# One visit a tile for the local attention jobs on TensorE, and ScalarE's activation moved to the head of a step, in a fused attention and feed-forward kernel

## The chip, the cores and the metric

The kernel runs on one core of one Trainium2 chip. The metric is the device time of one execution in microseconds (us), lower is better. Everything is computed in float32 precision: the large matmuls take each float32 operand as the sum of two float32r parts, a high one and the rest.

## The reference

Eight heads of sparse attention over eight sequences of 576 tokens, then a feed-forward layer over all 4608 tokens. The first four heads are local (a token sees itself and the 31 before it), the last four are strided (a token sees the earlier ones with the same position modulo 32).

```python
rel = pos[:, None] - pos[None, :]
mask_local = (rel >= 0) & (rel < 32)
mask_strided = (rel >= 0) & (pos[None, :] % 32 == pos[:, None] % 32)
masks = np.stack([mask_local if h < H // 2 else mask_strided for h in range(H)], axis=0)
scores = np.where(masks[None], (q @ k.transpose(0, 1, 3, 2)) / np.sqrt(D), -1e9)
attn = np.exp(scores - scores.max(-1, keepdims=True))
attn = attn / (attn.sum(-1, keepdims=True) + 1e-9)
x = (attn @ v).transpose(0, 2, 1, 3).reshape(B * S, H * D)      # 4608 x 512
h = x @ w_in                                                    # 512 x 2048
out = (0.5 * h * (1.0 + erf(h / np.sqrt(2.0)))) @ w_out         # 2048 x 512
```

## The kernel before

The tokens are cut into 12 tiles of 384, the feed-forward width into 16 blocks of 128. A step n is one tile and one block (n = 16 * tile + block, 192 steps). In a step `ffn_h(n)` issues 12 matmuls of 384 columns (4 channel groups, three products of high and low parts each: L602 to L604) into a PSUM tile `H`, of which there are two. `ffn_g(n)` makes the gate: the Gelu on ScalarE (L611, "the activation" below), a rounded copy `gh` on ScalarE (L613), and the rest `gl = H - gh` on VectorE (L615). `ffn_o(n - 2)` issues 9 matmuls of 512 columns (L641 to L643) into three PSUM banks. So TensorE runs H(n), O(n-2), H(n+1), O(n-1), H(n+2), and H(n+2) needs the bank of H(n), which is free once `gl` of step n is made.

The input x of a tile (`x_tile`: a high and a low part, two buffers) is made by attention while the tile before it is in the feed-forward. Its strided half comes from VectorE, row by row, in units of up to four rows: products of q and k (L477), maximum and subtraction (L485, L486), the exponential on ScalarE (L487), sums and quotients (L503 to L507), weighted sums of v (L517, L519), a transpose `xs` (L527). The units stand in one long list, `strided`; `run_strided(upto)` issues from it up to a cost given by the step, with the costs that stand beside each operation, so that a tile's units are done about two steps before the tile starts. An exponential is put on a list `exps` and issued by `flush_exps`, in the loop either at the unit's sum (`zsum`) or in the part of a local job that has exponentials of its own. A finished unit leaves a "split" on the list `splits`: a copy of `xs` into x's high part on ScalarE (L230) and the rest on VectorE (L232), in `to_x`.

The local half comes from three jobs a tile (`band_job`, parts 0 to 6, run by `part`): 0 scores (32 matmuls a job in the trace, L290) into the banks S0 and S1; 1 mask and row minimum on VectorE (L304); 2 four exponentials on ScalarE (L308); 3 sum, reciprocal, quotient and transpose on VectorE (L311 to L314) and eight small transfers into a band matrix; 4 values (16 matmuls a job, L328) into the bank X (the third job: S0); 5 and 6 `to_x`. `visit(n)` at the head of a step runs parts 0 and 1 of the three jobs in block 2 of a tile, parts 2 and 3 in the steps after it (a job every other step), and parts 4 to 6 in block 12, all for the next tile.

The first 16 steps are woven by hand with the loading of the weights and the first tiles' attention (`START`); the loop from step 16 on calls `step(n)`. In the loop the order on ScalarE and TensorE is that of the program; on VectorE, GpSimd and the transfer queue of SP a planner orders by its own estimate of when each instruction is ready.

Of the kernel before, what the change touches and what calls it, by code (L numbers as in the profile page):

```python
# [10 lines left out]
F32 = mybir.dt.float32  # L11
# [12 lines left out]
P = 128  # L24
STRIDE = 32
TT = 384
LU = 64
# [55 lines left out]
def attn_ffn_kernel(ctx: ExitStack, tc: tile.TileContext, qk, vl, qka, va, qs, ks, vs, w, out):  # L83
    nc = tc.nc
    NJ = qk.shape[0]
    NR, D = qs.shape[2:]
    S = NR * STRIDE
    HL = P // STRIDE
    NT, DM = out.shape
    NF = w.shape[0]  # L90
    NC = DM // P
    NU = len(PLACE)
    NV = len(VISITS)
    NTILE = NT // TT
    NS = NTILE * NF
    JPT = NJ // NTILE
    SC = 1.0 / (D ** 0.5)
    DH = D // 32
    N2 = HL // 2
# [11 lines left out]
    ps_a = ctx.enter_context(tc.tile_pool(name="ps_a", bufs=1, space=bass.MemoryType.PSUM))  # L111
# [8 lines left out]
    def rows(j):  # L120
        return slice(j * D, (j + 1) * D)
# [4 lines left out]
    def slot(name, shape, dtype=F32):  # L126

        return wpool.tile(shape, dtype, name=name, tag="w")
# [41 lines left out]
    def x_tile(t):  # L170
        if t not in xt:
            xt[t] = [xpool.tile([P, NC, TT], F32R, name=f"x{i}_{t}", tag=f"x{i}{t % 2}") for i in "hl"]
        return xt[t]


    jq, jv = {}, {}
# [8 lines left out]
    def load_jv(x):  # L185
        if x < NJ and ("v", x) not in loaded:
            loaded.add(("v", x))
            jv[x] = lpool.tile([LK, 2, HL, D], F32, name=f"vl_{x}", tag="vl", bufs=4)
            nc.sync.dma_start(jv[x], vl[x])
# [8 lines left out]
    def small(name):  # L198
        return [lpool.tile([P, 4], F32, name=f"{k}_{name}", tag=k, bufs=4) for k in ("nm", "ss", "rs")]
# [29 lines left out]
    def to_x(dh_, dl_, src):  # L229
        nc.scalar.copy(dh_, src)  # L230
        yield
        nc.vector.tensor_tensor(dl_, src, dh_.bitcast(F32), ALU.subtract)  # L232

    def local_job(x, banks=None, dve=0, pn=-1):
# [35 lines left out]
        dst = [a[:, 0:N2, c0:c0 + P] for a in x_tile(t)]  # L270
        yield from to_x(*dst, xv)

    def band_job(x, bt, sx=None):

        QB = STRIDE
        i = x % JPT if sx is not None else 0
        sx = {} if sx is None else sx
        if i == 0:  # L280
            sx["s"] = [ps_a.tile([P, DM], F32, name=f"S{j}_L{x}", tag=f"S{j}") for j in range(2)]
        s = [t[:, i * P:(i + 1) * P] for t in sx["s"]]
        qv = jq[x][:, 0:2 * N2 * LU].rearrange("p (r a t) -> p r a t", r=N2, a=2)
        kv = jq.pop(x)[:, 2 * N2 * LU:].rearrange("p (r a t) -> p r a t", r=N2, a=2)
        head = [(h % 2, slice(h // 2 * 2 * QB, (h // 2 + 1) * 2 * QB)) for h in range(HL)]
        for h in range(0, HL, 2):
            for g in range(P // QB):
                a, b = divmod(g, 2)
                for j in range(2):
                    nc.tensor.matmul(s[j][g * QB:(g + 1) * QB, head[h][1]],  # L290
                                     qv[rows(j), h // 2, a, b * QB:(b + 1) * QB],
                                     kv[rows(j), h // 2, a, b * QB:(b + 2) * QB],
                                     start=True, stop=True, tile_position=(j * D, g * QB))
        yield
        p1 = lpool.tile([P, 4 * LK], F32, name=f"P_L{x}", tag="P", bufs=2)
        p2 = lpool.tile([P, DM], F32, name=f"PT_L{x}", tag="PT", bufs=2)
        pb, pt = p2[:, 0:DM // 2], p2[:, DM // 2:]
        pv = pb.rearrange("p (c h t) -> p c h t", c=2, h=HL)
        nm, ss, rs = small(f"L{x}")
        first_ = [a for a in range(2) if LPLACE[2 * x + a][1] == 0]  # L300
        msk = bmask[first_[0] if first_ else None]
        for h in range(HL):
            j, cs = head[h]
            nc.vector.tensor_tensor_reduce(p1[:, h * 2 * QB:(h + 1) * 2 * QB], s[j][:, cs], msk, -SC, 3.0e38,  # L304
                                           ALU.add, ALU.min, nm[:, h:h + 1])
        yield
        for h in range(HL):
            nc.scalar.activation(pv[:, :, h, :], p1[:, h * 2 * QB:(h + 1) * 2 * QB].rearrange(  # L308
                "p (c t) -> p c t", c=2), AF.Exp, bias=nm[:, h:h + 1], scale=-1.0, accum_out=ss[:, h:h + 1])
        yield  # L310
        nc.vector.tensor_scalar_add(ss, ss, 1e-9)  # L311
        nc.vector.reciprocal(rs, ss)
        nc.vector.tensor_tensor(pv, pv, rs.unsqueeze(1).unsqueeze(3).to_broadcast([P, 2, HL, QB]), ALU.mult)
        nc.vector.transpose(pt, pb)  # L314
        tv = pt.rearrange("p (c q) -> p c q", c=2)
        for g in range(P // QB):
            for c in range(2):
                kb = g % 2 + c
                nc.sync.dma_start(bt[kb * QB:(kb + 1) * QB, g, :], tv[g * QB:(g + 1) * QB, c, :])
        yield  # L320
        if i % 2 == 0:
            sx["x"] = ps_a.tile([P, DM], F32, name=f"X_L{x}", tag="X" if i == 0 else "S0")
        xv = sx["x"][:, i % 2 * N2 * P:(i % 2 + 1) * N2 * P].rearrange("p (r q) -> p r q", r=N2)
        bv = bt.rearrange("p (a b) (h q) -> p a b h q", a=2, h=HL)
        for r in range(N2):
            for a in range(2):
                for j in range(2):
                    nc.tensor.matmul(xv[rows(j), r, a * LU:(a + 1) * LU], jv[x][:, a, 2 * r + j, :],  # L328
                                     bv[:LK, a, :, 2 * r + j, :], start=True, stop=True)
        jv.pop(x)  # L330
        load_jv(x + 3)
        yield
        t, c0 = divmod(x * P, TT)
        dst = [d[:, 0:N2, c0:c0 + P] for d in x_tile(t)]
        yield from to_x(*dst, xv)


    ka = {}
# [90 lines left out]
    for vi in range(NA, NV):  # L429
        n = VISITS[vi][2]  # L430
# [26 lines left out]
    exps, splits = [], []  # L457

    def flush_exps(u):
        while exps and exps[0][0] <= u:  # L460
            exps.pop(0)[1]()
# [132 lines left out]
    ready = [t * NF for t in range(NTILE)]  # L594
    xfree = [0, 0] + ready[1:-1]
# [58 lines left out]
    N0 = 17  # L654
    U0 = sum(x[4] <= NA for x in PLACE)
    for u in range(U0, NU + 1):
        for v, what, names in ((u, strided_qk, "qk"), (u - 1, strided_av, "v")):
            if U0 <= v < NU:
                vi, _, r0, nr, t, _ = PLACE[v]
# [3 lines left out]
    cum, last = [], [0.0] * NTILE  # L663
    tot = 0.0
# [6 lines left out]
    def run_strided(upto):  # L671
        while pos[0] < len(strided) and cum[pos[0]] <= upto + 1e-9:
            if strided[pos[0]][1] == 0.6 and len(splits) >= 3:
                break
            strided[pos[0]][2]()
            pos[0] += 1

    pbig = []
    t = slot("pbig", [P, 4 * DM])
# [35 lines left out]
    for i in range(JPT):  # L715
        t = opool.tile([P, DM], F32, name=f"first_{i}", tag="ob", bufs=3)
# [34 lines left out]
    with tc.manual_schedule(engines={ET.DVE, ET.Activation, ET.PE, ET.SP}):  # L751
        for it in START:
            kind = it[0]
            if kind in "wqvSBEe":
                x = int(it[1:] or 0)
# [12 lines left out]

    SCORES, VALUES = 2, 12
    score_at = {ready[t - 1] + SCORES: t for t in range(2, NTILE)}
    value_at = {ready[t - 1] + VALUES: t for t in range(2, NTILE)}
    banks = {}
    local = {}
    band = slot("band", [P, 4 * DM])
# [4 lines left out]
    def part(x, *which):  # L781

        for p in which:
            if p == 0:
                local[x] = [band_job(x, bts[x % NBT], banks), 0]
            assert local[x][1] == p
            local[x][1] += 1
            if next(local[x][0], True) is not None:
                load_jq(x + 3)

    def visit(n):

        for i in range(JPT):
            for d, p in ((1, 2), (2, 3)):
                t = score_at.get(n - 2 * i - d)
                if t is not None:
                    if p == 2:
                        flush_exps(NU)
                    part(t * JPT + i, p)
        if n in score_at:  # L800
            for p in (0, 1):
                for i in range(JPT):
                    part(score_at[n] * JPT + i, p)
        if n in value_at:
            for ps in ((4,), (5, 6)):
                for i in range(JPT):
                    part(value_at[n] * JPT + i, *ps)

    def step(n):
        c = n // NF  # L810
        while splits and n >= xfree[splits[0][0]]:
            for _ in splits.pop(0)[1]():
                pass
        visit(n)
        if c + 1 < NTILE:
            a, e = ready[c] + (1 if c == 0 else 0), ready[c + 1]
            need = last[c] + (last[c + 1] - last[c]) * min(1.0, max(0.0, (n - a + 1) / (e - a - 2)))
            run_strided(max(need, tot * (n - N0) / (ready[-1] - 2 - N0)))
        if NB <= n < NS:
            ffn_h(n)  # L820
            for _ in ffn_g(n):
                pass
        if n == NS + 1:
            ffn_o(n - 3, n - 2)
        elif n >= NB + 2 and n < NS:
            ffn_o(n - 2)
        if n >= NB + 2 and (n - 2) % NF == NF - 1:
            store((n - 2) // NF)

    with tc.manual_schedule(engines={ET.Activation, ET.PE}):  # L830
        for n in range(NB, NS + 1):
            step(n)
# [67 lines left out]
```

## Time and profile before

| | before |
|---|---|
| median of three runs | 886.04 us (886.02 to 887.12) |
| the profiled execution | 886.71 us, of which the span from first to last instruction 884.8 |
| granted TensorE clock, mean | 0.999 |
| TensorE matmul busy | 861.5 us, 97% of the span |
| VectorE busy | 713.9 us, 81% |
| ScalarE busy | 457.5 us, 52% |
| mean of one: Gelu (L611), its copy (L613), `gl` (L615) | 475, 480 and 554 ns |
| mean of one: `to_x` of a local job on ScalarE (L230), on VectorE (L232) | 376 and 417 ns |
| median from issue to landing: q and k of a job, a band transfer | 4.6 and 1.8 us |

A row of the timeline gives the start of an instruction in us from the span's start, its duration, engine, line, operation, what it writes and reads, and in brackets how long its engine sat idle before it and what ended that. Consecutive instructions of one kind are merged (x48). Matmuls overlap in their pipeline, so the pace of TensorE is read from the starts, not from the durations.

### The profile page before, as it was taken

To read this page: it belongs to the slowest core of one execution; us is meant where nothing else is said; L and a number is where in the kernel's file an instruction comes from. 1 tells how busy PE (TensorE), PEld (TensorE's weight loads), DVE (VectorE), ACT (ScalarE), POOL (GpSimd) and SP (SyncE) were. 2 spreads that over 40 slices of the span, in tenths; PEclk is the share of its full clock that TensorE was granted. 3 is DMA by queue.
4 is the path that set the end of the run, shared out by engine and by line. 5 is a ranking of instruction groups with operands and counts; after the bars stand their busy time and mean duration, and the time that the engine had idled before them with its cause. 6 is when DMAs were issued, how large, how long until landed. Compare 5 with 4: busy or idle time off the path is not lost.

```text
span 884.8 us, 19306 instructions
## 1 busy us (share of the span) xinstructions
PE 861.5 (97%) x5984; PEld 771.1 (87%) x5984; DVE 713.9 (81%) x4897; ACT 457.5 (52%) x975; POOL 17.9 (2%) x89
## 2 busy tenths in 40 slices
PE   5699999999999999999999999999999999999998
PEld 4488898989989889889898988988888998999997
DVE  5999899599969999849989969969979988675111
ACT  5999574256546357247336436436534632733222
POOL 5000100000000000000000000000000000000000
PEclk9999999999999999999999999999999999999999
DMA  9981420221030122102012122012113011100001
GB/s 335 343 342 36 148 85 16 81 82 46 28 134 14 60 71 77 34 21 97 21 66 87 40 75 87 14 54 82 60 34 108 13 60 37 27 20 1 36 1 36
DMA packets 34551, 66.66 MB, mean 75 GB/s; under 512 B 6800, under 2 KB 16528, under 8 KB 32400
## 3 DMA queue, kind: packets, MB, share of 16 engines
q1 hardware_dynamic: 34448, 65.43, 22.3%
q8 instruction: 47, 0.77, 0.3%
q14 instruction: 56, 0.46, 0.2%
HBM read 51.64 MB, written 9.44 MB: 69 GB/s over the span
## 4 chain that ended last, share of the span: by engine, by line
PE 92%; DVE 5%; POOL 1%; issue 1%; ACT 0%; DMA 0%; SPq 0%; POOLq 0%; DVEq 0%
PE H L602 15%; PE H L604 15%; PE O L642 15%; PE O L643 15%; PE H L603 15%; PE O L641 14%; PE X_L L328 2%; PE S_L L290 1%; DVE acc L519 1%; DVE ws L153 1%; DVE junk L477 1%; DVE w L163 0%; DVE ws L155 0%; DVE P_L L304 0%; POOL bmask L697 0%
## 5 line engine op out<-in xcount | busy, mean ns | idle before, releaser
L611 ACT ACTIVATE H<-H 128x384 f32<-128x384 f32 x192 | 91.2, 475 | 355.8 <-PE H L604 303.2
L602 PE MATMUL H<-xh,w 128*128 128x384 f32 x768 | 262.7, 342 | 2.4 <-ACT xh L230 1.2
L604 PE MATMUL H<-xh,w 128*128 128x384 f32 x768 | 260.7, 339 | 1.7 <-DVE w L163 1.7
L603 PE MATMUL H<-xl,w 128*128 128x384 f32 x768 | 259.6, 338 | 0.7 <-DVE xl L232 0.7
L519 DVE SCALAR_TENSOR_TENSOR acc<-sv,sc,acc 128x64 f32<-128x64 f32 x1158 | 253.8, 282 | 0.6
L643 PE MATMUL O<-w,gl 128*128 128x512 f32 x576 | 228.2, 396 | 0.0
L642 PE MATMUL O<-w,gh 128*128 128x512 f32 x576 | 227.9, 396 | 0.0
L641 PE MATMUL O<-w,gh 128*128 128x512 f32 x576 | 224.7, 390 | 0.0
L477 DVE CUSTOM_DVE_ANT_0 junk<-sq,sk 128x64 f32<-128x64 f32 x1290 | 209.7, 219 | 7.3 <-DMA sk<-in_ks_dram 7.3
L615 DVE TENSOR_TENSOR gl<-H,gh 128x384 fp32r<-128x384 f32 x192 | 106.4, 554 | 110.0 <-ACT gh L613 109.0
L602 PEld LDWEIGHTS H<-xh,w 128*128 128x128 f32 x768 | 145.3, 189 | 12.8 <-ACT xh L230 1.4
L603 PEld LDWEIGHTS H<-xl,w 128*128 128x128 f32 x768 | 145.3, 189 | 8.4 <-DVE xl L232 1.1
L604 PEld LDWEIGHTS H<-xh,w 128*128 128x128 f32 x768 | 145.1, 189 | 2.3 <-DVE w L163 2.2
L643 PEld LDWEIGHTS O<-w,gl 128*128 128x128 f32 x576 | 108.3, 188 | 23.1
L642 PEld LDWEIGHTS O<-w,gh 128*128 128x128 f32 x576 | 108.3, 188 | 18.2
L641 PEld LDWEIGHTS O<-w,gh 128*128 128x128 f32 x576 | 108.5, 188 | 17.5
L477 DVE DVE_READ_ACCUMULATOR2_ANT sc<- 128x1 f32 x1290 | 107.0, 83 | 0.0
L613 ACT CAST gh<-H 128x384 fp32r<-128x384 f32 x192 | 92.2, 480 | 6.0
L611 ACT ACT_TABLE_LOAD x47 | 60.3, 1283 | 0.8
L487 ACT ACT_TABLE_LOAD x35 | 44.9, 1283 | 0.6
L308 ACT ACTIVATE PT_L<-P_L,nm_L 128x64 f32<-128x64 f32 x132 | 44.0, 335 | 0.1
L517 DVE TENSOR_SCALAR acc<-sv,sc 128x64 f32<-128x64 f32 x132 | 26.5, 264 | 1.5 <-DMA sv<-in_vs_dram 1.2
(106 smaller groups left out, 500.0 us busy)
## 6 DMA issues: line engine op xcount, KB each, us to landing
ws<-in_w_dram SPq DMA_DIRECT2D x16, 1024.0 KB, 11.2
qk<-in_qk_dram SPq DMA_DIRECT2D x36, 320.0 KB, 4.6
out_dram<-ob SPq DMA_DIRECT2D x34, 256.0 KB, 2.5
vl<-in_vl_dram SPq DMA_DIRECT2D x36, 192.0 KB, 3.2
sk<-in_ks_dram SPq DMA_DIRECT2D x8, 576.0 KB, 4.6
sv<-in_vs_dram SPq DMA_DIRECT2D x8, 576.0 KB, 3.9
band<-PT_L SPq DMA_DIRECT2D x240, 16.0 KB, 1.8
sq<-in_qs_dram SPq DMA_DIRECT2D x4, 576.0 KB, 4.2
```

The source lines that it names most:

```text
L477: nc.vector.tensor_tensor_reduce(junk, sq[vi, "q"][:, r0 + r, :], sq[vi, "k"][:, c, :], 1.0, 0.0, ALU.mult, ALU.add, ss[u][:, r, c:c + 1])
L487: exps.append((u, lambda: nc.scalar.activation(s, s, AF.Exp, scale=SC)))
L519: nc.vector.scalar_tensor_tensor(acc[:, r, :], sq[vi, "v"][:, c, :], wgt, acc[:, r, :], ALU.mult, ALU.add)
L602: nc.tensor.matmul(hp, w1[f][:, 0, c, :], xh[:, c, :], start=(c == 0), stop=False)
L603: nc.tensor.matmul(hp, w1[f][:, 0, c, :], xl[:, c, :], start=False, stop=False)
L604: nc.tensor.matmul(hp, w1[f][:, 1, c, :], xh[:, c, :], start=False, stop=(c == NC - 1))
L611: nc.scalar.activation(hp, hp, AF.Gelu)
L613: nc.scalar.copy(gh, hp)
L615: nc.vector.tensor_tensor(gl, hp, gh.bitcast(F32), ALU.subtract)
L641: nc.tensor.matmul(o, gh[:, sl], w2[f][:, 0, :], start=(f == 0), stop=False)
L642: nc.tensor.matmul(o, gh[:, sl], w2[f][:, 1, :], start=False, stop=False)
L643: nc.tensor.matmul(o, gl[:, sl], w2[f][:, 0, :], start=False, stop=(f == NF - 1))
```

## The change

`visit(n)` now runs, in block 13 of a tile, part 4 (values) of the next tile's three jobs and right behind them part 0 (scores) of the three jobs of the tile after that; only the first loop tile's scores have a visit of their own. The third job's values go into the last 128 columns of the two banks that the scores behind them are about to fill. Parts 1 to 3 are spread over 11 steps, a job every four steps (every two for the first tile), and parts 5 and 6 follow in the step of the visit; all of these come from a new `softmaxes(n)`. In `step(n)` the H matmuls and the gate now stand ahead of the splits, the local jobs' parts, a `flush_exps` of every exponential outstanding, and the strided list; the strided list's pace is set to end one step earlier. The next q and k of a job are loaded at part 0 and not after part 6.

```diff
+    def score_banks(t):
+        return [ps_a.tile([P, DM], F32, name=f"S{j}_{t}", tag=f"S{j}") for j in range(2)]
...
-        if i == 0:
-            sx["s"] = [ps_a.tile([P, DM], F32, name=f"S{j}_L{x}", tag=f"S{j}") for j in range(2)]
-        s = [t[:, i * P:(i + 1) * P] for t in sx["s"]]
+        sx = {x // JPT: score_banks(x // JPT)} if sx is None else sx
+        s = [t[:, i * P:(i + 1) * P] for t in sx[x // JPT]]
...
-        if i % 2 == 0:
-            sx["x"] = ps_a.tile([P, DM], F32, name=f"X_L{x}", tag="X" if i == 0 else "S0")
-        xv = sx["x"][:, i % 2 * N2 * P:(i % 2 + 1) * N2 * P].rearrange("p (r q) -> p r q", r=N2)
+        if i == 0:
+            sx["x"] = ps_a.tile([P, DM], F32, name=f"X_L{x}", tag="X")
+
+        xv = [sx["x"][:, (N2 * i + r) * P:(N2 * i + r + 1) * P] if i < 2 else sx[x // JPT + 1][r][:, JPT * P:]
+              for r in range(N2)]
...
-        yield from to_x(*dst, xv)
+        if i < 2:
+            both = [(sx["x"][:, i * N2 * P:(i + 1) * N2 * P].rearrange("p (r q) -> p r q", r=N2), slice(0, N2))]
+        else:
+            both = [(xv[r], r) for r in range(N2)]
+        parts = [to_x(*[w_[:, d, c0:c0 + P] for w_ in x_tile(t)], src) for src, d in both]
...
-    SCORES, VALUES = 2, 12
-    score_at = {ready[t - 1] + SCORES: t for t in range(2, NTILE)}
-    value_at = {ready[t - 1] + VALUES: t for t in range(2, NTILE)}
+    FIRST, VISIT = 2, 13
+    value_at = {ready[t - 1] + VISIT: t for t in range(2, NTILE)}
+    score_at = {ready[1] + FIRST: 2, **{n: t + 1 for n, t in value_at.items()}}
+    soft_at = {}
+    for n, t in score_at.items():
+        for i in range(JPT):
+            for p in (1, 2, 3):
+                soft_at.setdefault(n + p + i * (2 if t == 2 else 4), []).append((t * JPT + i, p))
...
-            if next(local[x][0], True) is not None:
+            next(local[x][0], None)
+            if p == 0:
                 load_jq(x + 3)
...
+        t = value_at.get(n, 0)
         if n in score_at:
-            for p in (0, 1):
-                for i in range(JPT):
-                    part(score_at[n] * JPT + i, p)
-        if n in value_at:
-            for ps in ((4,), (5, 6)):
-                for i in range(JPT):
-                    part(value_at[n] * JPT + i, *ps)
+            banks[score_at[n]] = score_banks(score_at[n])
+        for i in range(JPT if t else 0):
+            part(t * JPT + i, 4)
+        for i in range(JPT if score_at.get(n, NTILE) < NTILE else 0):
+            part(score_at[n] * JPT + i, 0)
+
+    def softmaxes(n):
+
+        t = value_at.get(n, 0)
+        for i in range(JPT if t else 0):
+            part(t * JPT + i, 5, 6)
+        for x, p in soft_at.get(n, ()):
+            if x < NJ:
+                if p == 2:
+                    flush_exps(NU)
+                part(x, p)
 
     def step(n):
         c = n // NF
-        while splits and n >= xfree[splits[0][0]]:
-            for _ in splits.pop(0)[1]():
-                pass
         visit(n)
-        if c + 1 < NTILE:
-            a, e = ready[c] + (1 if c == 0 else 0), ready[c + 1]
-            need = last[c] + (last[c + 1] - last[c]) * min(1.0, max(0.0, (n - a + 1) / (e - a - 2)))
-            run_strided(max(need, tot * (n - N0) / (ready[-1] - 2 - N0)))
         if NB <= n < NS:
             ffn_h(n)
             for _ in ffn_g(n):
                 pass
+        old = len(splits)
+        while old and n >= xfree[splits[0][0]]:
+            for _ in splits.pop(0)[1]():
+                pass
+            old -= 1
+        softmaxes(n)
+        flush_exps(NU)
+        if c + 1 < NTILE:
+            a, e = ready[c] + (1 if c == 0 else 0), ready[c + 1]
+            need = last[c] + (last[c + 1] - last[c]) * min(1.0, max(0.0, (n - a + 1) / (e - a - 3)))
+            run_strided(max(need, tot * (n - N0) / (ready[-1] - 3 - N0)))
```

## Rows read from the trace of the kernel before

**Rows 1.** Timeline of PE around one values visit, from step 43 on

```profile
225.34 0.33 PE L602 MATMUL H<-xh,w 128*128 128x384 f32 x1
...
229.62 1.62 PE L328 MATMUL X_L<-band,vl 96*64 96x64 f32 x48
231.17 0.44 PE L602 MATMUL H<-xh,w 128*128 128x384 f32 x1
...
235.46 0.33 PE L602 MATMUL H<-xh,w 128*128 128x384 f32 x1
...
239.65 0.33 PE L602 MATMUL H<-xh,w 128*128 128x384 f32 x1
```

**Rows 2.** Timeline of PE around one scores visit, step 34

```profile
182.16 0.33 PE L602 MATMUL H<-xh,w 128*128 128x384 f32 x1
...
186.45 1.17 PE L290 MATMUL S_L<-qk 64*32 64x64 f32 x96
187.55 0.45 PE L602 MATMUL H<-xh,w 128*128 128x384 f32 x1
...
191.84 0.33 PE L602 MATMUL H<-xh,w 128*128 128x384 f32 x1
```

**Rows 3.** Timeline of PE in the opening: values and scores side by side

```profile
54.45 0.69 PE L328 MATMUL X_L<-first,vl 96*64 96x64 f32 x16
55.07 0.45 PE L290 MATMUL S_L<-qk 64*32 64x64 f32 x32
55.45 0.44 PE L602 MATMUL H<-xh,w 128*128 128x384 f32 x1
```

**Rows 4.** Timeline of PE in the opening: a job's values alone

```profile
93.91 0.69 PE L328 MATMUL X_L<-first,vl 96*64 96x64 f32 x16
94.52 0.50 PE L641 MATMUL O<-w,gh 128*128 128x512 f32 x1
```

**Rows 5.** Waits of the whole run: who waited for whom, us, times, longest

```profile
ACT xh L230 <- DVE xs L527: 14.3, 5, 6.4
...
DVE z L503 <- ACT sc L487: 12.4, 15, 1.1
...
PE H L602 <- DVE gl L615: 0.9, 1, 0.9
```

**Rows 6.** Timeline of ACT before and in the slow step 134

```profile
619.65 1.28 ACT L308 ACT_TABLE_LOAD   x1
...
623.69 0.47 ACT L611 ACTIVATE H<-H 128x384 f32<-128x384 f32 x1
...
631.08 0.41 ACT L230 CAST xh<-xs 128x256 fp32r<-128x256 f32 x1 [6.40 <-DVE xs L527]
631.39 0.47 ACT L611 ACTIVATE H<-H 128x384 f32<-128x384 f32 x1
```

**Rows 7.** Timeline of PE at its one wait, before step 136

```profile
626.64 0.33 PE L604 MATMUL H<-xh,w 128*128 128x384 f32 x1
...
628.90 0.33 PE L602 MATMUL H<-xh,w 128*128 128x384 f32 x1
...
634.17 0.44 PE L602 MATMUL H<-xh,w 128*128 128x384 f32 x1 [0.92 <-DVE gl L615]
...
638.46 0.33 PE L602 MATMUL H<-xh,w 128*128 128x384 f32 x1
```

**Rows 8.** Groups by line on ACT from 117 us on: busy, mean, idle before

```profile
L611 ACT ACTIVATE H<-H 128x384 f32<-128x384 f32 x175 | 83.1, 475 | 343.0 <-PE H L604 294.3 <-DVE sc L477 24.6 <-DVE acc L519 12.8
...
L487 ACT ACT_TABLE_LOAD x34 | 43.6, 1283 | 0.6
...
L308 ACT ACT_TABLE_LOAD x10 | 12.8, 1283 | 0.2
...
L487 ACT ACTIVATE sc<-sc 128x32 f32<-128x32 f32 (+9 forms) x34 | 8.1, 239 | 0.4
```

**Rows 9.** Busy time in one stretch of 70 us: PE, PEld, DVE, ACT, POOL

```profile
186.00:256.00 70.00, 70.00 (x482) 63.00 (x481) 66.74 (x551) 36.68 (x81) 0.66 (x5) 1.00 0.21 66
```

More of the change, by code (lines that the diff above doesn't have):

```diff
@@ L278, in band_job @@
         i = x % JPT if sx is not None else 0
-        sx = {} if sx is None else sx
-        if i == 0:
-            sx["s"] = [ps_a.tile([P, DM], F32, name=f"S{j}_L{x}", tag=f"S{j}") for j in range(2)]
-        s = [t[:, i * P:(i + 1) * P] for t in sx["s"]]
+        sx = {x // JPT: score_banks(x // JPT)} if sx is None else sx
+        s = [t[:, i * P:(i + 1) * P] for t in sx[x // JPT]]
         qv = jq[x][:, 0:2 * N2 * LU].rearrange("p (r a t) -> p r a t", r=N2, a=2)
@@ L327, in band_job @@
                 for j in range(2):
-                    nc.tensor.matmul(xv[rows(j), r, a * LU:(a + 1) * LU], jv[x][:, a, 2 * r + j, :],
+                    nc.tensor.matmul(xv[r][rows(j), a * LU:(a + 1) * LU], jv[x][:, a, 2 * r + j, :],
                                      bv[:LK, a, :, 2 * r + j, :], start=True, stop=True)
@@ L333, in band_job @@
         t, c0 = divmod(x * P, TT)
-        dst = [d[:, 0:N2, c0:c0 + P] for d in x_tile(t)]
-        yield from to_x(*dst, xv)
+        if i < 2:
[3 more added lines that the diff above has]
+        parts = [to_x(*[w_[:, d, c0:c0 + P] for w_ in x_tile(t)], src) for src, d in both]
+        for p in parts:
+            next(p)
+        yield
+        for p in parts:
+            next(p, None)
     ka = {}
@@ L787, in part @@
             local[x][1] += 1
-            if next(local[x][0], True) is not None:
+            next(local[x][0], None)
+            if p == 0:
                 load_jq(x + 3)
     def visit(n):
-        for i in range(JPT):
[L794 to L799, printed above, removed]
-        if n in score_at:
-            for p in (0, 1):
-                for i in range(JPT):
-                    part(score_at[n] * JPT + i, p)
-        if n in value_at:
-            for ps in ((4,), (5, 6)):
-                for i in range(JPT):
-                    part(value_at[n] * JPT + i, *ps)
+        t = value_at.get(n, 0)
+        if n in score_at:
+            banks[score_at[n]] = score_banks(score_at[n])
[12 more added lines that the diff above has]
+                part(x, p)
     def step(n):
         c = n // NF
-        while splits and n >= xfree[splits[0][0]]:
-            for _ in splits.pop(0)[1]():
-                pass
         visit(n)
-        if c + 1 < NTILE:
-            a, e = ready[c] + (1 if c == 0 else 0), ready[c + 1]
-            need = last[c] + (last[c + 1] - last[c]) * min(1.0, max(0.0, (n - a + 1) / (e - a - 2)))
-            run_strided(max(need, tot * (n - N0) / (ready[-1] - 2 - N0)))
         if NB <= n < NS:
```

## The prediction

> **What bounds the kernel now.** [...] From step 18 to the end a plain step takes 4.19 us (239.65 - 235.46 in [rows 1]), and only two things break the beat: the visits of the local jobs, and one wait. So a gain must come out of the visits or out of that wait; work on ScalarE and VectorE counts only where it makes TensorE wait. The chain of waits says the same: from the end back it is all TensorE's own matmuls, down to that one wait.
>
> A values visit: two steps take 235.46 - 225.34 = 10.12 us, 1.74 more than two plain ones. The 48 matmuls themselves run from 229.62 to 231.17, 1.55 us. So 0.19 us are edges, lost where TensorE changes between big and small matmuls [rows 1]. A scores visit: 191.84 - 182.16 = 9.68, so 1.30 more than plain, of which the 96 matmuls take 1.10 (186.45 to 187.55) and the edges 0.20 [rows 2]. The loop has ten visits of each kind.
>
> The wait: the list of waits has TensorE waiting once for VectorE's `gl` [rows 5]. The step starting at 628.90 and the next take 638.46 - 628.90 = 9.56, 1.18 more than plain [rows 7]. How it came about is on ScalarE: a split's copy waited 6.40 us for VectorE's transpose `xs`, and the activation queued behind it began at 631.39 [rows 6], while its last matmul was done at 626.64 + 0.33 = 626.97 [rows 7]: 4.4 us late.
>
> How much lateness is free: a step's H ends 2.26 us after it starts (626.97 against 628.90 - 4.19), and its bank is wanted two steps after it started, so 6.1 us after its end. Gelu, copy and `gl` take 475 + 480 + 554 ns, with the gaps some 1.6. So ScalarE and VectorE together may be 4.5 us late before TensorE notices. All steps but one stay under that.
>
> **One visit in place of two.** Values and scores stand side by side in 9 visits; the first scores and the last values stay alone. Each of the 9 saves one pair of edges, 0.20 us, if the change from values to scores in the middle costs nothing. The opening of the kernel has that very pair: 16 values matmuls from 54.45, 32 scores from 55.07, H at 55.45, so 0.62 and 0.38 us [rows 3]. Alone, 16 values took 0.61 (93.91 to 94.52) [rows 4], and a third of a scores visit is 1.10 / 3 = 0.37. The middle costs 0.02. What the opening doesn't show is scores going into banks that values have just been written to, as the third job's are now. So a merge is worth between 0 and 0.20; I take 0.18, by the nearest rows, the opening's: 9 x 0.18 = **1.6 us** (0 to 1.8).
>
> [...]
>
> **Activation first.** Around the loop, ScalarE's queue hardly changes: gate, splits, local parts, exponentials, gate. What changes is which step's VectorE work it meets, since the strided list of step n now stands behind `gl(n)` and not ahead of it, and is paced to end a step earlier for that. A split still stands behind the gate after the list that made it, so the waiting of [rows 6] is not excluded by construction. What changes is how late VectorE is then. Before, the mask and minimum of three jobs (12 operations) fall into the step of the scores, and quotients and transposes follow every other step; step 134 comes four steps after such a burst. Now a job comes every four steps. VectorE is busy 66.74 us of 70 in a full stretch [rows 9], so bursts are what makes it late. It also stood 12.4 us waiting for strided exponentials, 15 times, just ahead of their sums [rows 5]; issued a step after their subtraction, they are ready long before. The strided pace rises by 1 part in 157. I count the wait as gone: **1.2 us**; its bounds are 0 (it stays, or another of its size comes) and 1.2.
>
> **What is hidden.** The third job's `to_x` becomes two pairs, one for each bank: per tile at most 376 ns more on ScalarE and 417 ns on VectorE (nothing, if time goes with columns). VectorE has 3.3 us idle in its fullest stretch [rows 9], and x is wanted three steps, 12.6 us, after the visit. Without that cover it would be up to 4 us over ten tiles. The `to_x` copies no longer stand ahead of the activation in the visit's step.
>
> The local exponentials lose company: on the loop's 30 occasions only 10 had a table load of their own, the others shared one with a strided exponential issued together [rows 8]. Flushed every step, the 34 strided ones would meet them by chance in 34 x 30 / 157, some 6 or 7 steps. So 57 or 58 pairs of loads in place of 44, 13 x 2.57 = 34 us more on ScalarE, against 343 us that it idles before activations [rows 8]. In a step: a local job's load, four exponentials and load back take 623.69 - 619.65 = 4.04 us [rows 6], with the gate 5.0, so the next activation is 0.8 late; a strided one behind it takes 1.28 + 0.24 + 1.28 + 1.0 = 3.8 and gives 0.4 back. That is free under 4.5.
>
> [...]
>
> Transfers: the 30 loads of q and k move from part 6 to part 0, 16 steps ahead of use, and land in 4.6 us. On SP's queue they wait for the scores that free their buffer; behind them stand band transfers, whose data come three steps later. The last job's band leaves 11 steps after its scores and is wanted 5 steps (21 us) on; a transfer lands in 1.8 us. For the first tile it is 4 steps, as before. GpSimd's work stays as it is.
>
> **Sum.** 1.6 + 1.2 = 2.8 us. The profiled execution took 886.71, so 883.9 there; against the median of the runs, 886.04, the forecast is **883.2**. Steps before 18 and after 175 are unchanged.
>
> **The rivals.**
> - *The wait stays, or another of its size takes its place.* The order on VectorE is the planner's, and a new order may put another `xs` late. For it: the structure is the same, and splits met VectorE 5 times [rows 5]. 886.04 - 1.6 = 884.4.
> - *The merge saves nothing*, because scores into banks just written wait, or the middle costs an edge. Against it: [rows 3]. 886.04 - 1.2 = 884.8.
> - *ScalarE meets VectorE more often: slower.* The flush puts 34 exponentials, each waiting for its subtraction (L486), ahead of the next activation; before, they hardly waited (0.4 us in all [rows 8]), being issued a unit later. Each one caught behind a late VectorE holds the activation, as the split did, for 1.2 us. From four such waits on the kernel is 0.2% slower (4 x 1.2 = 4.8, less 2.8); with five it is 886.04 - 2.8 + 6.0 = 889.2. Against it: VectorE must be more than 4 us late, which one of 34 splits met.
> - *The table loads bind.* A local step of 5.0 and strided ones behind it would have to exceed 4.5 us of lateness. Were each load followed by an unseen pause of its own length, 1.28 us, the two steps would take 7.6 and 6.3 us, 5.5 more than two plain ones and 1.0 over what is free, at six or seven places: 886.04 - 2.8 + 6.5 = 889.7. The pause would show at [rows 6] and doesn't. [...]
>
> **How the numbers follow.** Forecast 0.57; wait stays 0.21; no saving by the merge 0.06; more waiting 0.14; loads 0.02. What a measurement can tell from no change is about 0.2%, 1.8 us: faster is below 884.3, slower above 887.8. Faster holds the forecast and, the edges being worth up to 1.8, a little of the second case: 0.60. Same holds the rest of that, the third, and the milder part of the fourth: 0.27. Slower: 0.13. The range runs from 882.3 (edges at 0.20, the wait gone, and 0.7 for runs that spread over 1.1 us, 886.02 to 887.12) to 886.8, where three waits have eaten the gain; it leaves out most of the last two cases.
>
> **What the changed profile would show.** Right: eleven visits in the loop, the merged ones 2.83 to 2.87 us over two plain steps, 48 matmuls and 96 with no gap; no wait of TensorE for `gl` after step 18; some 57 pairs of table loads; hardly a wait of the sums for exponentials. Wrong: H starts over 4.19 us apart outside the visits, with ScalarE's `sc` or `xh` waiting for VectorE right ahead of a late activation; or a gap between values and scores.

## The result, and the profile after

The changed kernel takes 888.21 us (median of 20 runs, 886.21 to 891.01) where the kernel before, run in turn on the same chip, takes 886.12 us (885.90 to 887.22). The ratio is 1.002, with an interval of 1.0014 to 1.0026: slower, by 2.1 us, where 883.2 us and a gain were forecast. The profiled execution took 889.66 us, 2.95 more than that of before.

I read the list of waits first. In the changed kernel the activation is L622, its copy `gh` L624, `gl` L626; H is L613 to L615, the strided products are L488, their weighted sums L528 and L530, `to_x` is still L230 and L232. From 117 us on (columns: who waited for whom, us in total, times, longest):

```profile
ACT xh L230 <- DVE xl L232: 39.1, 10, 8.3
...
DVE z L514 <- ACT sc L498: 18.7, 22, 1.0
...
PEld H L613 <- DVE gl L626: 5.1, 3, 3.0
...
PE H L613 <- DVE gl L626: 3.8, 3, 2.6
...
DVE junk L488 <- DMA sk<-in_ks_dram: 3.3, 2, 2.8
DVE acc L528 <- DMA sv<-in_vs_dram: 2.8, 2, 2.6
ACT xh L230 <- DVE xs L538: 1.5, 1, 1.5
```

Two things are new against [rows 5]. TensorE waits three times for `gl` and not once. And ScalarE's copies wait 39.1 us for VectorE's remainders `xl`, 10 times; over the whole of its loop before, that entry has 8.2 us. VectorE's waits for strided k and v that have not landed are not new. The same list of the kernel before has more of them:

```profile
DVE junk L477 <- DMA sk<-in_ks_dram: 7.3, 3, 3.7
...
DVE acc L517 <- DMA sv<-in_vs_dram: 1.2, 2, 0.9
```

TensorE waited for none of these. The longest is in step 29, the step that now has the first merged visit, and `gl` came 1.75 us late there:

```profile
168.79 0.23 DVE L477 CUSTOM_DVE_ANT_0 junk<-sq,sk 128x64 f32<-128x64 f32 x1 [3.68 <-DMA sk<-in_ks_dram]
```

In the changed kernel the wait in step 29 is shorter, 2.81 us, and `gl` comes 4.98 us late. So what matters is what stands beside such a wait. The wait of [rows 6] for `xs` is all but gone, but the sums wait longer for their exponentials than before, 18.7 us in 22 cases, not hardly at all.

A visit is named here by the tile whose x it completes; tile 2's visit is in step 29, while tile 1 is in the feed-forward. The timeline of TensorE shows two of the three waits behind tile 2's visit, a whole merged visit (231 to 242), and the third wait behind tile 9's:

```profile
175.56 0.44 PE L613 MATMUL H<-xh,w 128*128 128x384 f32 x1 [0.34 <-DVE gl L626]
...
180.92 0.45 PE L613 MATMUL H<-xh,w 128*128 128x384 f32 x1 [0.90 <-DVE gl L626]
...
231.25 0.33 PE L613 MATMUL H<-xh,w 128*128 128x384 f32 x1
...
235.53 1.15 PE L331 MATMUL X_L<-band,vl 96*64 96x64 f32 x32
236.51 0.64 PE L331 MATMUL S<-band,vl 96*64 96x64 f32 x16
237.08 1.17 PE L291 MATMUL S<-qk 64*32 64x64 f32 x96
238.18 0.44 PE L613 MATMUL H<-xh,w 128*128 128x384 f32 x1
...
242.47 0.33 PE L613 MATMUL H<-xh,w 128*128 128x384 f32 x1
...
661.47 0.33 PE L613 MATMUL H<-xh,w 128*128 128x384 f32 x1
...
668.40 0.45 PE L613 MATMUL H<-xh,w 128*128 128x384 f32 x1 [2.58 <-DVE gl L626]
...
669.27 0.52 PE L613 MATMUL H<-xh,w 128*128 128x384 f32 x1
...
670.23 0.52 PE L613 MATMUL H<-xh,w 128*128 128x384 f32 x1
```

The merged visit costs 242.47 - 231.25 = 11.22 us for two steps, 2.84 more than two plain ones of 4.19: 48 values in 1.55 us (235.53 to 237.08), 96 scores in 1.10, nothing between them. A values visit and a scores visit took 1.74 and 1.30 more [rows 1, 2], so each of the nine merges saves 0.20, 1.8 in all.

The loss is in four steps. Starts of H lie 4.68 and 5.36 us apart at the first two waits, 6.93 at the third, and the step after the third takes 5.79 as well: 0.49 + 1.17 + 2.74 + 1.60 = 6.0 us over plain steps. With 1.8 saved and the wait of before gone (1.2), that makes 3.0 more; the two profiled executions differ by 2.95.

The 1.60 is no wait. After the idle time the H matmuls start 0.32 us apart (three of them from 669.27 to 670.23), where a plain step has some 0.175 (12 in 2.1 us, from 231.25 to the first O matmul at 233.35). The profile's windows (columns: window and length; busy time of PE, PEld, DVE, ACT, POOL; granted clock; DMA share, GB/s):

```profile
661.40:665.60 4.20, 4.20 (x22) 3.63 (x21) 1.62 (x21) 0.00 (x0) 0.00 (x0) 1.00 0.55 188
665.60:668.40 2.80, 0.22 (x2) 0.00 (x1) 2.80 (x25) 0.00 (x0) 0.00 (x0) 1.00 0.00 0
668.40:670.30 1.90, 1.90 (x7) 1.90 (x8) 1.90 (x15) 1.17 (x5) 0.00 (x0) 0.59 0.00 0
670.30:672.20 1.90, 1.90 (x8) 1.90 (x7) 1.90 (x17) 0.41 (x1) 0.00 (x0) 0.52 0.04 9
672.20:674.20 2.00, 2.00 (x11) 1.64 (x10) 2.00 (x18) 1.80 (x3) 0.00 (x0) 1.00 0.00 0
```

Behind TensorE's wait of 2.58 us the granted clock was 0.59 and then 0.52, for 3.8 us in all, where it had been 1.00. Behind the wait of 0.92 in the kernel before [rows 7] it stayed at 1.00.

Why `gl` was late at 668 us is on the other two engines. ScalarE, with the copies behind the second one left out:

```profile
659.58 0.47 ACT L622 ACTIVATE H<-H 128x384 f32<-128x384 f32 x1 [3.20 <-PE H L615]
660.09 0.48 ACT L624 CAST gh<-H 128x384 fp32r<-128x384 f32 x1
660.47 0.38 ACT L230 CAST xh<-X_L 128x256 fp32r<-128x256 f32 x1
669.10 0.37 ACT L230 CAST xh<-X_L 128x256 fp32r<-128x256 f32 x1 [8.25 <-DVE xl L232]
...
669.68 0.51 ACT L622 ACTIVATE H<-H 128x384 f32<-128x384 f32 x1
```

And VectorE, the strided products and most weighted sums left out:

```profile
654.14 0.55 DVE L626 TENSOR_TENSOR gl<-H,gh 128x384 fp32r<-128x384 f32 x1
...
665.19 0.74 DVE L528 TENSOR_SCALAR acc<-sv,sc 128x64 f32<-128x64 f32 x4 [2.58 <-DMA sv<-in_vs_dram]
...
667.79 0.56 DVE L626 TENSOR_TENSOR gl<-H,gh 128x384 fp32r<-128x384 f32 x1
...
668.65 0.42 DVE L232 TENSOR_TENSOR xl<-X_L,xh 128x256 fp32r<-128x256 f32 x1
```

ScalarE was in time: H of this step ended soon before 659.58, and `gh` was done at 660.57. VectorE took it up at 667.79, 7.2 us later. The groups of VectorE between those two `gl` say what it did instead:

```profile
L488 DVE CUSTOM_DVE_ANT_0 junk<-sq,sk 128x64 f32<-128x64 f32 x31 | 4.7, 219 | 0.0
L530 DVE SCALAR_TENSOR_TENSOR acc<-sv,sc,acc 128x64 f32<-128x64 f32 x21 | 4.7, 277 | 0.0
...
L528 DVE TENSOR_SCALAR acc<-sv,sc 128x64 f32<-128x64 f32 x4 | 0.7, 251 | 2.6 <-DMA sv<-in_vs_dram 2.6
```

VectorE runs in the order that the planner gave it, and in that order 31 products and 25 weighted sums stand ahead of this `gl`, and among them one that waits 2.58 us for v. By their starts (0.146 us for a product, 0.195 for a weighted sum) that work is about 9.4 us. I took the same sum, over all of VectorE's work, for every step of tiles 2 to 9: ahead of the `gl` of a visit's step (block 13) stand 8.1 us in the median (7.0 to 9.9), ahead of the other blocks' at most 4.4, and before the change no block had a median over 5.6. The visit's step is long (6.93 us from H to H), so the queue does not grow from tile to tile, but each time this `gl` comes 2.5 us late in the median, where others come about 1 late.

What is queued behind it then suffers. The first copy of the visit's values needs VectorE only for its remainder `xl`, but that stands behind the late `gl`; the second job's copy waits for that remainder, 8.25 us; and the next activation stands behind the copy, at 669.68. Both jobs' values lie in bank X, and ScalarE's copies out of it wait 39.1 us for remainders in the ten visits, once in each; the 20 copies of the third job, out of the banks of the scores, wait for none. Why a copy out of bank X waits for a remainder out of the same bank, no run shows.

### The profile page after: what moved, and what is told of

Its sections match the earlier page's. It is cut to its first block, busy times and chain, and to the rows that moved or that the text cites. A ratio compares the mean times of both kernels' runs of the same rounds, so it can differ in the third digit from the quotient of the medians.

```text
span 887.9 us, 19419 instructions
## 1 busy us (share of the span) xinstructions
PE 861.0 (97%) x5984; PEld 772.5 (87%) x5984; DVE 717.4 (81%) x4907; ACT 490.4 (55%) x1011; POOL 17.8 (2%) x89
## 4 chain that ended last, share of the span: by engine, by line
PE 88%; DVE 7%; DMA 2%; issue 1%; POOL 1%; SPq 0%; ACT 0%; POOLq 0%; DVEq 0%
PE H L613 15%; PE H L615 14%; PE H L614 14%; PE O L653 14%; PE O L654 14%; PE O L652 14%; DVE acc L530 2%; DVE junk L488 1%; PE X_L L331 1%; PE S L291 1%; DVE ws L153 1%; DMA sk<-in_ks_dram 1%; DMA sv<-in_vs_dram 1%; DVE gl L626 0%; DVE w L163 0%
## 5 line engine op out<-in xcount | busy, mean ns | idle before, releaser
L622 ACT ACTIVATE H<-H 128x384 f32<-128x384 f32 x192 | 91.6, 477 | 329.9 <-PE H L615 296.5
L613 PE MATMUL H<-xh,w 128*128 128x384 f32 x768 | 262.6, 342 | 4.5 <-DVE gl L626 3.8
L615 PE MATMUL H<-xh,w 128*128 128x384 f32 x768 | 261.4, 340 | 2.0 <-DVE w L163 2.0
L530 DVE SCALAR_TENSOR_TENSOR acc<-sv,sc,acc 128x64 f32<-128x64 f32 x1158 | 252.9, 282 | 0.6
L488 DVE CUSTOM_DVE_ANT_0 junk<-sq,sk 128x64 f32<-128x64 f32 x1290 | 205.9, 221 | 3.3 <-DMA sk<-in_ks_dram 3.3
L626 DVE TENSOR_TENSOR gl<-H,gh 128x384 fp32r<-128x384 f32 x192 | 106.4, 554 | 107.5 <-ACT gh L624 106.6
L613 PEld LDWEIGHTS H<-xh,w 128*128 128x128 f32 x768 | 145.8, 190 | 15.4 <-DVE gl L626 5.1
L615 PEld LDWEIGHTS H<-xh,w 128*128 128x128 f32 x768 | 145.7, 190 | 2.5 <-DVE w L163 2.5
L488 DVE DVE_READ_ACCUMULATOR2_ANT sc<- 128x1 f32 x1290 | 109.7, 85 | 0.0
L624 ACT CAST gh<-H 128x384 fp32r<-128x384 f32 x192 | 92.2, 480 | 6.0
```

Of the source, the lines that this page charges most:

```text
L488: nc.vector.tensor_tensor_reduce(junk, sq[vi, "q"][:, r0 + r, :], sq[vi, "k"][:, c, :], 1.0, 0.0, ALU.mult, ALU.add, ss[u][:, r, c:c + 1])
L530: nc.vector.scalar_tensor_tensor(acc[:, r, :], sq[vi, "v"][:, c, :], wgt, acc[:, r, :], ALU.mult, ALU.add)
L613: nc.tensor.matmul(hp, w1[f][:, 0, c, :], xh[:, c, :], start=(c == 0), stop=False)
L615: nc.tensor.matmul(hp, w1[f][:, 1, c, :], xh[:, c, :], start=False, stop=(c == NC - 1))
L622: nc.scalar.activation(hp, hp, AF.Gelu)
L624: nc.scalar.copy(gh, hp)
```

## The experiments

Each was timed in turn with the kernel before, which took 886.12, 885.89 and 885.96 us in the three groups of runs. I name the theories once, with the letters that some expectations use. *Chain* (A; E, where it needs nothing besides the pile): the copies through bank X carry VectorE's lateness into the next activation. *Bunched loads* (B): the local q, k and v loads, all issued in the visit, hold up strided k and v. *Order* (C): the new order of the step costs, the merge gains. *Pile* (D): the 8 us that stand ahead of the visit's `gl` make it late, and TensorE notices when a strided load or the chain comes on top. Where no unit stands, times are us.

**Order alone.** From the kernel before: visits stay apart, in blocks 2 and 12, but `step(n)` gets the changed kernel's sequence. The edit is shortened to its calls, in their order:

```diff
-        while splits and n >= xfree[splits[0][0]]: ...
         visit(n)                      # parts 0 and 4 alone
-        run_strided(max(need, tot * (n - N0) / (ready[-1] - 2 - N0)))
         if NB <= n < NS: ffn_h(n); ffn_g(n)
+        splits; softmaxes(n); flush_exps(NU)
+        run_strided(max(need, tot * (n - N0) / (ready[-1] - 3 - N0)))
```

> The new order of a step alone: gate first, then splits, local parts and the flush; the two visits a tile (blocks 2 and 12) and the loads stay as before. Theory A (at the merged visit ScalarE's copy of the second job waits for VectorE's remainder of the first, ahead of the next gate, while VectorE has some 8 us of work between two gl): the copies stand ahead of the next gate here too, but VectorE's work at block 12 is shorter, so the waits are smaller; 885.5 to 887.5. Theory B (the loads of q, k and v bunched at the visit hold up the strided k and v that VectorE waits for): 885 to 886.5, the old wait of 1.2 gone or not. Theory C (the new order is what costs, the merge gains): 888 or more.

Measured 885.48 (884.95 to 885.78), ratio 0.999 (0.9981 to 0.9999). The old wait is gone, TensorE waits once for 0.22. ScalarE's copies wait for `xl` here too, 22.9 us in ten waits, the longest 5.4, at no cost to TensorE. So the order does not cost; it gains 0.6, which is near the limit of what can be told, and the theory of the order falls.

**Merge alone.** The changed kernel with the old sequence of the step, shortened in the same way:

```diff
+        splits
         visit(n)
-        if NB <= n < NS: ffn_h(n); ffn_g(n)
-        splits; softmaxes(n); flush_exps(NU); run_strided(...)
+        softmaxes(n); run_strided(...)
+        if NB <= n < NS: ffn_h(n); ffn_g(n)
```

> The merged visit alone (block 13, jobs spread over 11 steps, loads at part 0), with the old order of a step: splits, visit, local parts, strided list, then H and the gate. Theory A: the copies stand ahead of the gate of the visit's own step, with the same chain through VectorE, so waits at the visit remain in part: 885 to 888. Theory B: the loads are bunched as in the change, so about 888. Theory C: 883 to 884.5.

Measured 893.94 (892.94 to 895.18), ratio 1.0087 (1.0073 to 1.0101). No theory had this. The split stands ahead of the activation again, as in [rows 6], and in the same step as there, 134, its `xs` comes 10.1 us late. The copy on ScalarE, TensorE, and the windows after (columns as above):

```profile
636.93 0.41 ACT L230 CAST xh<-xs 128x256 fp32r<-128x256 f32 x1 [10.12 <-DVE xs L538]
```

```profile
640.02 0.69 PE L613 MATMUL H<-xh,w 128*128 128x384 f32 x1 [3.79 <-DVE gl L626]
```

```profile
641.00:644.00 3.00, 3.00 (x11) 3.00 (x10) 1.48 (x12) 2.24 (x3) 0.14 (x1) 0.50 0.00 0
```

TensorE's other wait, 3.13, is before step 26. Both lie outside the visits (steps 29, 45 and so on); behind those no step is slow. So with the old sequence the old wait grows, for a reason I did not follow, and the changed kernel's loss, behind the visits, is in neither edit alone. Behind the wait of 3.79 the granted clock is 0.50.

**One copy.** The values of jobs 0 and 1, side by side in bank X, are moved by one copy of 512 columns and one remainder, so that no copy out of the bank stands behind a remainder.

```diff
...
+        elif i == 0:
+            parts = []
+        elif i == 1:
+            parts = [to_x(*[w_[:, 0:N2, c0 - P:c0 + P].rearrange("p r (i q) -> p r i q", i=2) for w_ in x_tile(t)],
+                          sx["x"].rearrange("p (i r q) -> p r i q", i=2, r=N2))]
...
```

> The change, but the first two jobs of a tile, which share bank X, are brought into x by one copy of 512 columns and one remainder in place of two each, so ScalarE doesn't wait for VectorE between them. Theory A: ScalarE's 39 us of waiting for xl go, the gate after the visit is on time, and 2 to 4 us come back: 884 to 886. Theory B: the waits of VectorE for its loads stay and with them the time: 887.5 to 888.5.

Measured 887.44 (886.18 to 888.81), ratio 1.0011 (1.0003 to 1.002). The wait of `xh` for `xl` has left the list, and the chain with it; TensorE waits three times all the same (lines of this kernel stand six higher, `gl` is L632):

```profile
PE H L619 <- DVE gl L632: 2.3, 3, 1.7
```

The chain is a part of the loss, some 0.8 (the intervals overlap), and not its main cause. The 12 H matmuls behind the wait of 1.70 take 2.22 us to the first O matmul (666.56 to 668.78), as those behind the wait of 0.92 in the kernel before do (2.21), against 2.1 in a plain step: the pace stayed.

**Loads spread.** q, k and v of a job are loaded at its part 3 and not all in the visit.

```diff
-            if p == 0:
+            if p == 3:
+                load_jv(x)
                 load_jq(x + 3)
```

> The change, but the next q and k of a job and its v are loaded in its part 3, one job at a time, 3 to 11 steps after the visit, and not all six at the visit. Theory A: VectorE's waits for strided k and v shrink, the chain through the copies stays: 886.5 to 888. Theory B: the 2.6 and 2.8 us waits go and the stalls with them: 883.5 to 885.5.

Measured 888.03 (886.56 to 889.67), ratio 1.0022 (1.0013 to 1.003). VectorE still waits 2.96 for strided k at tile 2's visit and 1.26 for v at tile 9's, and the time is the changed kernel's. Bunching is not the cause.

**No reload.** Strided k and v are loaded for the first two groups of visits only; the later strided work reads those again, so that part of the attention is computed from other data. It is meant to take the load waits away and to leave order and pile.

```diff
+        if nm != "q" and gr in order_g[2:]:
+            for vi in first_of[gr]:
+                sq[vi, nm] = kept[nm][:, groups[vi][1]:groups[vi][1] + VISITS[vi][2]]
+            return
```

> The change, but the strided k and v of the last six visits of the list are not loaded: VectorE reads those of the visit before them (so that part of the attention is computed from other data). VectorE has no transfer to wait for. Theory D (at the merged visit VectorE's order holds some 8 us of work before the gate's gl, against 3.3 elsewhere, so gl is 2.5 to 3.7 us late there; that is free, until a wait of 2 to 3 us for a strided load stands in the same stretch, and then TensorE waits): 883 to 884.5, no wait of TensorE at the visits. Theory E (the 8 us and the chain of copies are enough by themselves): 886 or more.

Measured 885.17 (884.70 to 886.11), ratio 0.9991 (0.9982 to 1.0): 3.0 less than the changed kernel, and between the forecasts of D and E. The pile is still there, some 8 us. At tile 9's visit TensorE loses 0.55 where it lost 2.74 + 1.60. Tile 2's stays as it was, because there the load of q takes the place of k's (lines four higher):

```profile
171.16 0.22 DVE L492 CUSTOM_DVE_ANT_0 junk<-sq,sk 128x64 f32<-128x64 f32 x1 [2.79 <-DMA sq<-in_qs_dram]
```

So the load waits, in the place where the pile stands, are most of the loss, 3.0 of the 5.0 us over the forecast. Without the pile, as before the change, they cost nothing.

**Visit in block 10**, and the same with one copy: to see whether the place of the visit matters.

```diff
-    FIRST, VISIT = 2, 13
+    FIRST, VISIT = 2, 10
-                soft_at.setdefault(n + p + i * (2 if t == 2 else 4), []).append((t * JPT + i, p))
+                soft_at.setdefault(n + p + i * (1 if t == 2 else 4), []).append((t * JPT + i, p))
```

> The change with the merged visit in block 10 in place of 13 (the first tile's jobs one step apart in place of two, to be ready). The loads of strided k and v are still waited for in blocks 13 and 14 of the same tiles, now three steps after the visit. Theory D: the two don't meet, VectorE is as late at the visit as before, TensorE doesn't wait: 883 to 885. Theory E: the place doesn't matter, 886.5 to 888.5.

> Visit in block 10, and one copy into x for the two jobs that share a bank. Theory D: as the visit in block 10 alone, and the gate after the visit on time too: 883 to 884.5, below both kernels. Theory E: 885 to 887.

Measured 899.8 (899.46 to 902.54) and 898.56 (896.51 to 899.7). Both are inconclusive: the first tile's jobs now lie a step apart, and there ScalarE waits 7.6 for transfers out of the buffer that its exponentials write, the values wait for the band, and TensorE once 5.7 for `gl`. That hides in the time what was to be seen. The trace shows one thing in both: the pile goes with the visit. By the sum of above, ahead of `gl` stand 7.4 us (7.1 in the second run) in block 10, in the median, and 3.9 (3.8) in block 13. From the first of the two:

```profile
ACT L309 <- DMA band<-PT_L: 7.6, 1, 7.6
PE H L613 <- DVE gl L626: 6.0, 2, 5.7
```

**VectorE in order.** The changed kernel with VectorE, too, in the program's order in the loop.

```diff
-    with tc.manual_schedule(engines={ET.Activation, ET.PE}):
+    with tc.manual_schedule(engines={ET.DVE, ET.Activation, ET.PE}):
```

> The change, but VectorE's order in the loop is that of the program and not the planner's: nothing of the strided list of the visit's step stands ahead of its gl. Theory D: the work before gl at the visit falls from 8 to some 3.5 us, VectorE idles there and is early for gl, so a load's wait in that step has over 4 us of room: 883 to 886, if VectorE, 66 of 70 us busy a tile, can afford to idle some 2.8 us a tile; if not, it falls behind at the end of the list, over 888. Theory E: the chain of copies stays, 886 or more.

Measured **883.28** (882.87 to 883.51), ratio 0.9968 (0.9956 to 0.9981). It beats both kernels and is the forecast's time. TensorE waits for `gl` nowhere from 117 us on, VectorE for no transfer, and the sums' wait for exponentials is gone. The same visit of tile 9, on VectorE:

```profile
651.58 0.55 DVE L626 TENSOR_TENSOR gl<-H,gh 128x384 fp32r<-128x384 f32 x1
...
658.17 0.56 DVE L626 TENSOR_TENSOR gl<-H,gh 128x384 fp32r<-128x384 f32 x1 [3.11 <-ACT gh L624]
658.65 0.41 DVE L232 TENSOR_TENSOR xl<-X_L,xh 128x256 fp32r<-128x256 f32 x1
```

On ScalarE, and in the list of waits:

```profile
658.04 0.38 ACT L230 CAST xh<-X_L 128x256 fp32r<-128x256 f32 x1
659.10 0.37 ACT L230 CAST xh<-X_L 128x256 fp32r<-128x256 f32 x1 [0.68 <-DVE xl L232]
```

```profile
ACT xh L230 <- DVE xl L232: 6.7, 10, 0.7
```

VectorE now idles 3.11 us ahead of the `gl` that came 7.2 late, and between those two `gl` it does 15 weighted sums and nothing else (31 products and 25 sums in the changed kernel).

**Pile by hand.** To tell the pile from everything else that the program's order changes: the kernel above, with the pile put back. In a visit's step, that step's own strided list and three quarters of the next one's are issued ahead of H and the gate, so that some 8.3 us of VectorE's work stand ahead of `gl`. By the trace, nothing new stands ahead of the visit's activation on ScalarE.

```diff
         visit(n)
+        if n in value_at:
+            run_strided(upto(n + 0.75))
         if NB <= n < NS:
```

> The change in program order (883.28), with the pile put back by hand: in the step of a values visit the strided list runs 1.75 steps further ahead of the gate, some 8 us of VectorE's work before gl in place of 3. Theory D: gl is late by 2.5 to 5 us at the visits and TensorE waits at some of them, most where a load's wait falls in: 884.5 to 888. If the pile is harmless: 883.3.

Measured 886.07 (884.64 to 887.49), ratio 0.9993 (0.9984 to 1.0002): 2.8 more than without the pile. TensorE waits for `gl` four times, the longest at 320.83, and the load of v falls into the pile once more, the copies wait again:

```profile
PE H L613 <- DVE gl L626: 2.1, 4, 1.4
```

```profile
314.22 0.26 DVE L528 TENSOR_SCALAR acc<-sv,sc 128x64 f32<-128x64 f32 x1 [1.81 <-DMA sv<-in_vs_dram]
314.39 0.55 DVE L626 TENSOR_TENSOR gl<-H,gh 128x384 fp32r<-128x384 f32 x1
```

```profile
315.63 0.37 ACT L230 CAST xh<-X_L 128x256 fp32r<-128x256 f32 x1 [5.49 <-DVE xl L232]
```

A pile ahead of the visit's `gl` is enough to bring the waits back.

**VectorE in order in the kernel before, and with the new order alone.** Does the program's order gain without the merge? In both, the third job's masked scores also get a buffer of their own.

```diff
-        p1 = lpool.tile([P, 4 * LK], F32, name=f"P_L{x}", tag="P", bufs=2)
+        p1 = (lpool.tile([P, 4 * LK], F32, name=f"P_L{x}", tag="P", bufs=2) if i < 2 else
+              lpool.tile([P, 8 * QB], F32, name=f"P_L{x}", tag="P2", bufs=1))
-    with tc.manual_schedule(engines={ET.Activation, ET.PE}):
+    with tc.manual_schedule(engines={ET.DVE, ET.Activation, ET.PE}):
```

> The kernel before with VectorE's order in the loop that of the program (the third job's masked scores get a buffer of their own, without which that order would block itself). If program order is good by itself, its one wait goes: 884.5 to 885.3. If program order gains only where the planner's pile is, 886 to 890. Either way the merged visit's 1.7 us are missing, so it is slower than the change in program order (883.3).

> The new order of a step, visits apart as before, VectorE in program order (third job's buffer as in the other). Against the change in program order (883.28) it lacks the merge alone. If the merge is worth nine pairs of edges: 883.3 + 1.7 = 885.0. If the merge is worth nothing, 883.3.

Measured 885.36 (885.12 to 885.99), ratio 0.9992 (0.9983 to 1.0), and 884.95 (884.79 to 885.45), ratio 0.9986 (0.9977 to 0.9995). The kernel before has little to gain from VectorE's order. Between 884.95 and 883.28 stand the merge and what comes with it (the visit's block, the spread of parts 1 to 3, the place of the loads, and not the extra buffer): 1.67 us, against a forecast of 1.6. TensorE waits for `gl` in neither, and from the start of step 18 to that of the last step it takes 753.56 and 751.68 us; the 1.88 between them lie in the visits' steps, so the merge is the likely whole of it.

**In order in the visits' steps alone.**

```diff
+            if n in value_at:
+                with tc.manual_schedule(engines={ET.DVE, ET.Activation, ET.PE}):
+                    step(n)
```

> The change, with VectorE in program order in the ten steps with a values visit alone, the planner's elsewhere. Theory D (the pile of work ahead of gl in the visit's step is the cause): the work before gl there is 3 us again and TensorE doesn't wait: 883 to 884.5. If program order helps for another reason, or everywhere a little: 886 to 888.

Measured 900.31 (897.87 to 902.15), ratio 1.0154: a miss. The planner reorders what lies around the fixed steps; 5.2 us still stand ahead of the visit's `gl` in the median, and new waits come elsewhere, among them TensorE's for copies of the output (8.6 us in two cases) and exponentials that wait for their subtraction (13.8 us in seven cases), the mechanism of my third rival. It says nothing about the pile.

## Why the prediction was wrong

**What held.** The visit: 2.84 over plain steps, forecast 2.83 to 2.87, no gap in the middle, so the opening's pair [rows 3] was a fair measure, and the scores, 1.10 us for 96 as when they stood apart, did not wait for the banks just written. Its worth, 1.67 with VectorE in order. The old wait is gone. The table loads, from 117 us on, are the 57 pairs forecast, and outside the steps right behind a visit no activation began more than 1.5 us after its H:

```profile
L622 ACT ACT_TABLE_LOAD x57 | 73.1, 1283 | 1.0
L498 ACT ACT_TABLE_LOAD x34 | 43.6, 1283 | 0.6
L309 ACT ACT_TABLE_LOAD x23 | 29.5, 1283 | 0.4
```

**The step that failed** is "Activation first", where it says: "What changes is how late VectorE is then", and ends "I count the wait as gone". The old wait went, but VectorE did not get more punctual. I argued from its bursts in the program, two in place of one, and not from the order in which its queue would stand, which the planner makes anew. In the merged visit's step it puts 8.1 us of strided work ahead of `gl`, where the other blocks have at most 4.4. That alone is about what the 4.5 us of free lateness bear (0.55 lost at tile 9's visit when nothing was reloaded); with a load of k or v inside it that lands 2.6 to 2.8 us late it is not, and the chain of copies passes the lateness on to the next activation. The prediction put these load waits at nothing without a word, though the list of before has 7.3 us of them; they were harmless only as long as no pile stood beside them. The runs show each link: without the load waits 3.0 us come back, without the chain perhaps 0.8, with VectorE in order 4.9 (888.21 - 883.28), and with the pile put back by hand 2.8 are lost again.

**The rivals.** The first was nearest: "another of its size takes its place", by a new order of the planner's. It was priced at 1.2 us, the size of the old wait. The profiled execution has 4.4 in the steps of three waits and 1.6 more from the clock, which no part of the sum had. The third rival foretold a slower kernel, but its mechanism, exponentials that wait for their subtraction, is not in the changed kernel's list of waits. No run shows the pause of 1.28 us after a table load that the fourth supposes: in the changed kernel, from 673.35 on, two loads of 1.28 us and four exponentials take 4.05 us up to the next activation.

**Sums and exponentials.** "Hardly a wait" was wrong under the planner's order (18.7 us, 22 times) and right under the program's.

**What stays open.** Why the planner piles work in this step I only argue: the visit makes the step 2.8 us longer, and its estimate sees room there. That the changed kernel's runs spread over 4.8 us, those of before over 1.3, fits waits that hang on when a load lands, and the lower granted clock behind the longer ones (0.59 to 0.50 behind 2.58 and 3.79 us); I did not follow it run by run. Each trace is of one execution. A second buffer for strided k and v, which would let their loads start earlier, was not tried; neither was another block for the visit without the confusion in the first tile.

## What to carry to other kernels

A merge on the engine that bounds the kernel was worth what its rows said, and was lost on VectorE, which is idle for 19% of the span, since what counts there is what stands ahead of the one operation that is waited for. Where a scheduler orders a nearly full engine, a changed step means a new order: read, before counting a wait as gone, how many us of other work and which loads stand ahead of that operation, and if the order in the program is already the one wanted, try that engine in program order. Free lateness is one account for all causes: 4.5 us nearly bore the pile, and not the pile with a late load on top.

## What the runs showed of the hardware that I had not expected

A wait on TensorE cost more than its length here. Behind idle times of 2.58 and 3.79 us the granted clock was lower, 0.59 and 0.52 in the first case and 0.50 in the second; in the first the H matmuls behind the wait started 0.32 us apart, where a plain step has some 0.175, and 1.6 us were lost beyond it. Behind 0.92 [rows 7] and 1.70 (one copy) the pace stayed, with 2.21 and 2.22 us for the 12 H matmuls. Why the clock fell no run shows.
